# A long DFT in an fp32 kernel: the second transform of real and imaginary spectra as 64 x 64 products on quarters of TensorE, with mirrored sums in the outer steps

## Chip, cores, metric

One core of one Trainium2 chip. The metric is the device time of one execution in microseconds (us), the median of several executions. A "step" below is one block of 128 tokens of the main loop, which takes them in pairs; there are 196 steps, and I mark time by the start of each step's exponential on ScalarE.

## The reference

```python
X = np.fft.rfft(x, axis=1)                    # x: 8 x 3136 x 256, fp32
Y = X * (filt_r + 1j * filt_i)[None]
y = np.fft.irfft(Y, n=3136, axis=1)           # then 25088 tokens of 256
h = y @ w_in                                  # 256 -> 1024
sm = exp(h - max(h)) / (sum + 1e-9)
solu = h * sm
ln = (solu - mean) / sqrt(var + 1e-6) * g_ln
out = ln @ w_out                              # 1024 -> 256
```

The kernel does the length 3136 transform as 49 x 64: a first step over 49 rows (product `pa`), a second over 64 columns (`pb`), a product with the filter, and the way back (`pc`, then `py`). Entries 0 and 1 are transformed before the main loop. The other six are transformed in its gaps, in groups, while the loop does the two dense layers (`m` and `o`).

## The kernel before

Cuts are marked.

```python
# first step, entries 0 and 1: 16 tiles of x, 98 rows of 4 KB each, as 96 + 2 rows
def by_16(dmas, out, in_):
    n = out.shape[0] // 16 * 16
    dmas[0](out=out[:n], in_=in_[:n]);  dmas[1](out=out[n:], in_=in_[n:])
split((nc.sync.dma_start, nc.sync.dma_start), self.xs[i][0:NR],
      x[...].rearrange("(r n) c -> r n c", n=NH)[:, NCH * ch:NCH * ch + NCH, :])
# ...
def forward(self, i, ps):      # one residue s: 128 x 128 product, real and imaginary rows together
    nc.tensor.matmul(out=ps[:, ...], lhsT=self.des[i][:, j, 0, :], rhs=t2[...], start=True, stop=True)
def turn(self, i):             # ScalarE: swap the halves for the complex product
    nc.scalar.mul(turned[0:NQ], ps[NQ:P], -1.0);  nc.scalar.copy(out=turned[NQ:P], in_=ps[0:NQ])
def multiply(self, i, parts):  # VectorE: p = pb*f0 ; i = i*f1 ; p = p + i
# ... inverse: one 128 x 128 product into ps_t, one eviction by ScalarE
# after entries 0 and 1: ten products that nothing reads, so that TensorE's clock stays up
for j in range(10):
    nc.tensor.matmul(out=idle[:, 0, :], lhsT=tables[NS // NG - 1][:, 0, 0, :], rhs=last...)
# main loop: a unit of group n at step t
early[t]: forward, turn        products[0][t+1], products[1][t+1]: multiply
late[t + 1]: inverse           stores[t + 2]: store
```

PSUM in the main loop: `ps_b` one bank for pb, `ps_t` two for pa, py and pc, `ps_m` three for m, `ps_o` two for o.

Of the kernel before, what the change touches and what calls it, by code (L numbers as in the profile page):

```python
# [1 line left out]

# [15 lines left out]
P = 128  # L18
# [3 lines left out]

N1, N2 = 49, 64
NH = N2 // 2
NS, NQ = (N1 + 1) // 2, 64
NR = 2 * N1
NK = 4 * NS
NG = 5
# [10 lines left out]
    ((2,), (0, 6), (9, 13)),  # L39
    ((3, 4), (6, 13), (22, 25)),  # L40
# [6 lines left out]
def dft_tables():  # L47





    n1, n2 = np.arange(N1), np.arange(N2)
    s, q = np.arange(NS), np.arange(NQ)
    ph = 2 * np.pi * (np.outer(n1, s) % N1) / N1
    w = np.stack([np.cos(ph), -np.sin(ph)], 1)
    v = np.stack([2 * np.cos(ph), -2 * np.sin(ph)], 0)
    v[0, :, 0], v[1, :, 0] = 1.0, 0.0
    wf = np.zeros((N1, 2, NS, 2, 2))
    wi = np.zeros((NS, 2, 2, N1, 2))  # L60
    for h in range(2):
        wf[:, h, :, :, h] = w.transpose(0, 2, 1)
        wi[:, :, h, :, h] = v.transpose(2, 0, 1) / S

    kap = np.where(q[:, None] < 32, s + N1 * q[:, None], s + N1 * (95 - q[:, None]))
    sg = np.where(q < 32, 1.0, -1.0)[:, None]
    th = 2 * np.pi * ((n2[:, None, None] * kap) % S) / S
    c, sn = np.cos(th), np.sin(th)
    d = np.zeros((2, N2, NS, 2, NQ))
    d[0, :, :, 0] = c.transpose(0, 2, 1)  # L70
    d[1, :, :, 0] = sn.transpose(0, 2, 1)
    d[0, :, :, 1] = (-sn * sg).transpose(0, 2, 1)
    d[1, :, :, 1] = (c * sg).transpose(0, 2, 1)
    d = d.reshape(2 * N2, NS, 2 * NQ)
    f32 = np.float32
    de = np.stack([d, d.transpose(2, 1, 0)], 2)
    return wf.reshape(NR, NK).astype(f32), wi.reshape(NK, NR).astype(f32), de.astype(f32)


@with_exitstack  # L80
def kernel(
# [27 lines left out]
    f_dram = dram.tile([NS, NQ, 2, C], FP32, name="f_dram")  # L109
# [27 lines left out]
    def filter_rows(filt, quarter, s0, n):  # L137

        off, step = (s0 * C, C) if quarter % 2 == 0 else ((N1 - s0) * C, -C)
        return bass.AP(tensor=filt.tensor, offset=filt.offset + off,  # L140
                       ap=[[N1 * C, 32], [step, n], [1, C]])

# [3 lines left out]
    def by_16(dmas, out, in_):  # L146

        n = out.shape[0] // 16 * 16
        dmas[0](out=out[:n], in_=in_[:n])
        dmas[1](out=out[n:], in_=in_[n:])  # L150

    class Spectrum:



        def __init__(self, n, pools, load, load_de):
            self.n, self.entries, self.pools = n, GROUPS[n][0], pools
            self.load, self.load_de = load, load_de
            self.units = ([(s, 1) for s in range(NS)] if len(self.entries) == 2 else
                          [(s, min(2, NS - s)) for s in range(0, NS, 2)])  # L160
            self.xs, self.t1s, self.t2s, self.fs, self.prods, self.gs, self.des, self.turned = (
                {} for _ in range(8))

        def columns(self, ap, s, count):

            if len(self.entries) == 2:
                return ap[:, s, :, :].rearrange("b p c -> p b c")
            return ap[0, s:s + count, :, :].rearrange("s p c -> p s c")

        def fetch_x(self, i, split=by_16):  # L170
            b, ch = divmod(i, NH // NCH)
            self.xs[i] = self.pools["r"].tile([P, NCH, C], FP32, name=f"x_{self.n}_{i}", tag="r")
            split((nc.sync.dma_start, nc.sync.dma_start), self.xs[i][0:NR],
                  x[self.entries[b]].rearrange("(r n) c -> r n c", n=NH)[
                      :, NCH * ch:NCH * ch + NCH, :])
# [17 lines left out]
        def fetch(self, i, dma):  # L193
            s, count = self.units[i]
            cols = len(self.entries) * count
            self.t2s[i] = self.pools["t2"].tile([P, 2, C], FP32, name=f"t2_{self.n}_{i}", tag="t2")
            dma(out=self.t2s[i][:, 0:cols, :],
                in_=self.columns(d1[self.n], s, count))
# [7 lines left out]
        def forward(self, i, ps):  # L206
            s, count = self.units[i]
            t2, w = self.t2s.pop(i), len(self.entries)
            for j in range(count):
                nc.tensor.matmul(out=ps[:, w * j:w * j + w, :], lhsT=self.des[i][:, j, 0, :],  # L210
                                 rhs=t2[:, w * j:w * j + w, :], start=True, stop=True)
            self.prods[i] = ps

        def turn(self, i, **bufs):

            s, count = self.units[i]
            cols = len(self.entries) * count
            ps = self.prods[i][:, 0:cols, :]
            turned = self.pools["p"].tile([P, 2, C], FP32, name=f"i_{self.n}_{i}", tag="i",
                                          **bufs)[:, 0:cols, :]  # L220
            nc.scalar.mul(turned[0:NQ], ps[NQ:P], -1.0)
            nc.scalar.copy(out=turned[NQ:P], in_=ps[0:NQ])
            self.turned[i] = turned

        def multiply(self, i, parts):


            s, count = self.units[i]
            cols = len(self.entries) * count
            f = self.fs[i]  # L230

            def part(k):
                fk = f[:, 0:count, k, :]
                return fk.broadcast_to([P, cols, C]) if cols > count else fk

            if 0 in parts:
                pt = self.pools["p"].tile([P, 2, C], FP32, name=f"p_{self.n}_{i}", tag="p")[:, 0:cols, :]
                nc.vector.tensor_tensor(out=pt, in0=self.prods[i][:, 0:cols, :], in1=part(0), op=ALU.mult)
                self.prods[i] = pt
            if 1 in parts:  # L240
                turned, pt = self.turned.pop(i), self.prods[i]
                nc.vector.tensor_tensor(out=turned, in0=turned, in1=part(1), op=ALU.mult)  # L242
                nc.vector.tensor_tensor(out=pt, in0=pt, in1=turned, op=ALU.add)
                del self.fs[i]

        def inverse(self, i, evac):
            s, count = self.units[i]
            w = len(self.entries)
            pt, de = self.prods.pop(i), self.des.pop(i)
            ps = ps_t.tile([P, 2, C], FP32, name=f"pc_{self.n}_{i}", tag="t")  # L250
            for j in range(count):
                nc.tensor.matmul(out=ps[:, w * j:w * j + w, :], lhsT=de[:, j, 1, :],  # L252
                                 rhs=pt[:, w * j:w * j + w, :], start=True, stop=True)
            self.gs[i] = gt = self.pools["g"].tile([P, 2, C], FP32, name=f"g_{self.n}_{i}", tag="g")
            evac(out=gt[:, 0:w * count, :], in_=ps[:, 0:w * count, :])

        def store(self, i, dma):
            s, count = self.units[i]
            gt, cols = self.gs.pop(i), len(self.entries) * count
            dma(out=self.columns(d2[self.n], s, count), in_=gt[:, 0:cols, :])  # L260
# [569 lines left out]
```

## Time and profile before

| | before |
|---|---|
| median | 1786.94 us (1781.92 to 1788.27) |
| span of the profiled run, mean granted clock | 1779.0 us, 0.979 |
| first pb / idle products / first exponential | 70.4 / 141.0 / 194.5 us |
| steps 0 to 20, 20 to 94, 94 to 140 | 208.6, 620.8, 361.8 us |
| moved by DMA | 314.57 MB |

Up to 70 us x comes in and the first step runs; from 70 to 141 us VectorE does the complex products of entries 0 and 1; after that the main loop fills TensorE more and more.

### The profile page before, as it was taken

The page shows a single profiled execution, that of the slowest core. Times are in us where ns is not written, and L with a number is a line of the kernel's source. Part 1 is how long each engine was busy: PE and PEld are TensorE (multiplying, and loading weights), DVE is VectorE, ACT ScalarE, POOL GpSimd, SP SyncE. Part 2 cuts the span into 40 slices and gives each one's busy share as a digit, 9 for nine tenths or more (in the row PEclk, how much of TensorE's full clock was granted, in tenths as well). Part 3 has the DMA queues.
Part 4 walks back from the last instruction along what each step waited for, and adds up shares of the span by engine and source line. Part 5 has one row for each costly group of instructions (what it writes and reads, how often), then busy time and mean ns, then how long its engine had stood idle before and what let it go on. Part 6 is the DMA issues. An engine that isn't in the chain of part 4 may idle for free.

```text
span 1779.0 us, 28627 instructions
## 1 busy us (share of the span) xinstructions
PE 1671.6 (94%) x8692; PEld 1141.3 (64%) x8692; DVE 1244.1 (70%) x2586; ACT 1068.4 (60%) x1917; POOL 1093.9 (61%) x1290
## 2 busy tenths in 40 slices
PE   6688887899999999999999999989999999999996
PEld 1225445676666666766667667767777777777776
DVE  0793654578877875678798766767767777777773
ACT  2365555566767666666667666656666566655551
POOL 3242354677767775667877656546666656676664
PEclk9789998999999999999999999999999999999999
DMA  9876687897788865566777665557776444444443
GB/s 279 259 253 184 207 216 197 245 247 211 201 240 231 223 173 158 135 188 188 195 188 200 156 153 157 139 141 186 192 188 158 113 116 114 120 106 107 104 114 94
DMA packets 358120, 314.57 MB, mean 177 GB/s; under 512 B 60833, under 2 KB 318882, under 8 KB 357968
## 3 DMA queue, kind: packets, MB, share of 16 engines
q1 hardware_dynamic: 295664, 187.23, 41.0%
q0 software_dynamic: 29152, 86.45, 16.3%
q10 hardware_dynamic: 33152, 39.07, 7.7%
q8 instruction: 71, 1.16, 0.3%
q14 instruction: 81, 0.66, 0.1%
HBM read 131.65 MB, written 81.50 MB: 120 GB/s over the span
## 4 chain that ended last, share of the span: by engine, by line
PE 74%; DMA 11%; DVE 6%; ACT 3%; issue 3%; SPq 1%; POOL 1%; ACTq 0%; POOLq 0%; DVEq 0%
PE o L612 28%; PE m L500 28%; PE py L277 6%; PE pa L183 4%; PE pb L210 4%; PE pc L252 3%; DMA t<-d 2%; DMA x<-in_x_dram 2%; DMA d<-t 2%; DVE h L548 1%; DMA solu_t<-turn 1%; DMA f<-f_dram 1%; DMA de<-de_tbl 1%; ACT e L532 1%; DVE i L242 1%
## 5 line engine op out<-in xcount | busy, mean ns | idle before, releaser
L550 ACT ACTIVATE e<-h,nmu 128x1024 f32<-128x1024 f32 x196 | 225.3, 1150 | 307.9 <-DVE h L548 305.7
L612 PE MATMUL o<-w_out_sb,solu_t 128*128 128x128 f32 x3136 | 401.9, 277 | 3.0 <-DVE ot L629 1.9
L612 PEld LDWEIGHTS o<-w_out_sb,solu_t 128*128 128x128 f32 x3136 | 382.1, 193 | 33.6 <-issue 28.5
L500 PE MATMUL m<-w_in_sb,s 128*128 128x512 f32 x784 | 397.3, 598 | 6.3 <-ACT h L510 6.3
L612 PEld LDWEIGHTS o<-w_out_sb,u 128*128 128x128 f32 x2352 | 306.5, 192 | 148.7 <-issue 115.7
L612 PE MATMUL o<-w_out_sb,u 128*128 128x128 f32 x2352 | 312.7, 276 | 9.0 <-ACT ot L624 7.7
L479 POOL TENSOR_TENSOR u<-solu_t 128x512 f32<-128x512 f32 x98 | 153.9, 1571 | 265.8 <-DMA solu_t<-turn 152.3
L500 PE MATMUL m<-w_in_sb,y 128*128 128x512 f32 x588 | 304.5, 601 | 6.3 <-DVE h L521 3.5
L548 DVE SCALAR_TENSOR_TENSOR h<-e,rsum,h 128x1024 f32<-128x1024 f32 x196 | 291.8, 1489 | 7.1 <-DVE rsum L545 0.3
L631 DVE SCALAR_TENSOR_TENSOR ot<-o,rs_t,ot 128x128 f32<-128x128 f32 x294 | 102.5, 349 | 257.3 <-ACT ot L624 216.6
L479 POOL TENSOR_TENSOR u<-solu_t,u 128x512 f32<-128x512 f32 x98 | 144.7, 1477 | 173.1 <-PE o L612 171.6
L558 DVE STREAM_TRANSPOSE turn<-h 128x1024 f32<-128x1024 f32 x196 | 242.2, 1236 | 1.5
L524 DVE CUSTOM_DVE_ANT_0 h<-m,h 128x512 f32<-128x512 f32 x196 | 134.8, 688 | 138.3 <-ACT h L510 89.8
L510 ACT COPY h<-m 128x512 f32<-128x512 f32 x294 | 173.0, 589 | 91.3 <-PE m L500 77.9
L532 ACT ACTIVATE e<-h,nmax 128x1024 f32<-128x1024 f32 x196 | 224.5, 1146 | 0.0
L500 PEld LDWEIGHTS m<-w_in_sb,s 128*128 128x128 f32 x784 | 130.6, 192 | 79.2 <-issue 74.2
L277 PEld LDWEIGHTS py<-wi_t,t 100*128 100x128 f32 x1024 | 133.3, 195 | 62.9 <-issue 39.8
L183 PE MATMUL pa<-x,wf_t 98*100 98x512 f32 x256 | 141.7, 662 | 26.6 <-DMA x<-in_x_dram 20.7
L479 POOL TENSOR_TENSOR solu_t<-solu_t,solu_t 128x512 f32<-128x512 f32 x98 | 157.0, 1602 | 7.7
L277 PE MATMUL py<-wi_t,t 100*128 100x98 f32 x1024 | 134.9, 277 | 15.2 <-DMA t<-d 10.4
L500 PEld LDWEIGHTS m<-w_in_sb,y 128*128 128x128 f32 x588 | 99.3, 192 | 74.2 <-issue 50.8
L280 ACT COPY y<-py 128x392 f32<-128x392 f32 x128 | 108.2, 845 | 56.2 <-PE py L277 54.6
(72 smaller groups left out, 2049.1 us busy)
## 6 DMA issues: line engine op xcount, KB each, us to landing
solu_t<-turn SPq DMA_DIRECT2D x784, 128.0 KB
d<-g POOLq DMA_DIRECT2D x99, 256.0 KB, 5.5
out_dram<-ot SPq DMA_DIRECT2D x196, 128.0 KB
t<-d SPq DMA_DIRECT2D x56, 400.0 KB
d<-t POOLq DMA_DIRECT2D x96, 200.0 KB, 4.8
t<-d ACTq DMA_DIRECT2D x74, 256.0 KB
x<-in_x_dram SPq DMA_DIRECT2D x48, 392.0 KB
f<-f_dram POOLq DMA_DIRECT2D x104, 128.0 KB, 4.2
```

What stands on the lines that cost most here:

```text
L183: nc.tensor.matmul(out=ps[0:NK, j], lhsT=wf_t, rhs=self.xs[i][0:NR, 2 * u:2 * u + 2, :], start=True, stop=True)
L277: nc.tensor.matmul(out=psv[:, i, :], lhsT=t4s[e, ch][:, i, cb * P:cb * P + P], rhs=wi_t, start=True, stop=True)
L280: evac(out=y[:, cb, t0:t0 + S].rearrange("p (r n) -> p n r", n=NH)[:, n0:n0 + NCH, :], in_=psv)
L479: nc.gpsimd.tensor_tensor(out=out, in0=in0, in1=in1, op=op)
L500: nc.tensor.matmul(out=ms[j, bank], lhsT=lhsT, rhs=w_in_sb[:, w, :], start=m in (1, 2, 7), stop=True, skip_group_check=True)
L510: nc.scalar.copy(out=h_half(k, i), in_=ms[j, 0])
L524: nc.vector.tensor_tensor_reduce(out=h_half(k, i), in0=ms[j, bank], in1=h_half(*kept), scale=1.0, scalar=sofar, op0=ALU.add, op1=ALU.min, ...
L532: nc.scalar.activation(out=e, in_=hs[k], func=AFT.Exp, bias=nmaxs.pop(k)[:, 1:2], scale=-1.0, accum_out=esum)
L548: nc.vector.scalar_tensor_tensor(out=solu, in0=e, scalar=rsum, in1=solu, op0=ALU.mult, op1=ALU.mult, accum_out=nmu)
L550: nc.scalar.activation(out=e, in_=solu, func=AFT.Square, bias=nmu, scale=-float(DFF), accum_out=variances[g][:, i:i + 1])
L558: nc.vector.transpose(out=turns[g][:, :, i, :], in_=solus.pop(k).rearrange("p (f j) -> p f j", j=32))
L612: nc.tensor.matmul(out=pos[p, bank], lhsT=lhs[:, f, :], rhs=w[:, f, :], start=f == 0 and m in (1, 2, 7), stop=True, skip_group_check=True)
```

## The change

Intent: the second transform splits into real and imaginary inputs and outputs which only need 64 x 64 blocks when n2 is centred, so half of TensorE's work on it vanishes. Two residues are held as one unit, each of four quarters of the array does a 64 x 64 product at once, real and imaginary spectra go to two PSUM banks, and no turning on ScalarE is needed. To make n2 symmetric, the first step pairs column n with column 63 - n, so half of x is read mirrored.

Shortened; cuts are marked, and the last part names the calls without their arguments.

```diff
-                split((nc.sync, nc.sync), xs[0:NR], x....rearrange("(r n) c -> r n c")[:, 4ch:4ch+4])
+            for h, first, step in ((0, NCH * ch, C), (1, N2 - 1 - NCH * ch, -C)):
+                split(dmas, xt[N1 * h:N1 * h + N1],          # engines=15: 45 + 4 rows, twice
+                      bass.AP(..., offset=first * C, ap=[[N2 * C, N1], [step, NCH], [1, C]]))
...
+        def forward(self, i, pss):
+            for u in range(self.shape(i)[0]):        # residue: which half of the columns
+                for r in range(2):                   # real or imaginary: which half of the rows
+                    block = slice(NQ * r, NQ * r + NQ)
+                    self.product(i, pss[r][NQ * u:NQ * u + NQ], lambda v: de[block, v, 0, u, :],
+                                 t2[block, self.slots(u), :])
...
+            nc.vector.tensor_tensor(out=out, in0=re, in1=fk(part), op=ALU.mult)
+            nc.vector.tensor_tensor(out=term, in0=im, in1=fk(1 - part), op=ALU.mult)
+            add(out=out, in0=out, in1=term, op=(ALU.subtract, ALU.add)[part])
...  entries 0 and 1
+            sp.multiply(i, 0, nc.vector.tensor_tensor)
+            sp.multiply(i, 1, nc.gpsimd.tensor_tensor)
...
-            nc.tensor.matmul(out=idle[:, 0, :], lhsT=tables[NS // NG - 1][:, 0, 0, :],
+                             lhsT=tables[0][0:NQ, 0, 0]...,        # 64 rows
...  main loop: one pair of banks for pb and pc; m2 shares the banks of pa and py
+    ps_b = [pool(f"ps_b{u}", 1, PSUM) for u in range(2)]
...
+            early[t].append(forward into psum_pair("pb"))
+            late[t].append(multiply(i, 0, nc.vector.tensor_tensor))
+            products[t + 1].append(multiply(i, 1, nc.vector.tensor_tensor))
+            late[t + 1].append(inverse into psum_pair("pc"))
```

## The prediction

> **What bounds the kernel now.** I read the page first (busy shares), then the windows of 50 us, then the timeline of TensorE inside a full window, then the groups by form, and last the waits and the chain. The page, and two rows of its slices:
>
> ```profile
> PE 1671.6 (94%) x8692; PEld 1141.3 (64%) x8692; DVE 1244.1 (70%) x2586; ACT 1068.4 (60%) x1917; POOL 1093.9 (61%) x1290
> ...
> PE   6688887899999999999999999989999999999996
> ...
> DMA  9876687897788865566777665557776444444443
> ```
>
> TensorE (PE) is full from about the ninth slice (355 us) to the end, and not before, where the DMA engines are the fuller ones. The windows say it in numbers:
>
> ```profile
> 50.00:100.00 50.00, 35.27 (x62) 11.05 (x60) 44.59 (x82) 23.42 (x37) 15.78 (x24) 0.81 0.83 255
> ...
> 300.00:350.00 50.00, 45.28 (x216) 30.73 (x216) 29.73 (x56) 29.41 (x54) 29.80 (x40) 0.96 0.94 259
> ...
> 500.00:550.00 50.00, 50.00 (x255) 33.19 (x254) 37.73 (x77) 34.90 (x64) 36.39 (x45) 1.00 0.85 238
> ```
>
> The columns are PE, PEld, DVE, ACT, POOL, then clock, DMA share, GB/s. From 67 to 141 us (first and last pb and pc of entries 0 and 1) VectorE is the bound: 44.6 of 50 us. From 200 to 350 us transfers are. After 350 us PE is busy throughout. Busy time overlaps in pipelined matmuls, so I take costs from the starts in the timeline of PE:
>
> ```profile
> 461.28 1.02 PE L210 MATMUL pb<-t,de 128*128 128x512 f32 x2
> 462.14 1.95 PE L612 MATMUL o<-w_out_sb,solu_t 128*128 128x128 f32 x16
> 463.92 1.02 PE L500 MATMUL m<-w_in_sb,s 128*128 128x512 f32 x2
> 464.78 1.02 PE L500 MATMUL m<-w_in_sb,y 128*128 128x512 f32 x2
> 465.64 1.05 PE L612 MATMUL o<-w_out_sb,u 128*128 128x128 f32 x8
> 466.53 1.06 PE L612 MATMUL o<-w_out_sb,solu_t 128*128 128x128 f32 x8
> ```
>
> An fp32 product of 512 columns is two passes (x2), and the next starts 462.14-461.28 = 0.86 us later. A 128-column product is 0.89/4 = 0.22 us. A pair of steps needs 7 x 0.86 + 28 x 0.22 = 12.2 us, times 98 = 1200 us. In the window 500 to 550 all starts times these costs fill 97 to 98% of it. There, what PE saves or pays goes nearly one for one into the end time. The products under change, by form:
>
> ```profile
> L210 PE MATMUL pb<-t,de 128*128 128x512 f32 x150 | 82.2, 633 | 14.4 <-DMA t<-d 9.5 <-DVE p L238 4.7
> L252 PE MATMUL pc<-p,de 128*128 128x512 f32 x150 | 80.5, 620 | 10.8 <-DVE p L243 7.4 <-ACT g L255 3.5
> ...
> L210 PE MATMUL pb<-t,de 128*128 128x256 f32 x100 | 26.9, 391 | 9.8 <-issue 7.2 <-DMA de<-de_tbl 2.6
> L252 PE MATMUL pc<-p,de 128*128 128x256 f32 x100 | 25.9, 379 | 0.0
> ```
>
> So 75 products of 512 columns and 50 of 256, each way. 25 of the 75 belong to entries 0 and 1, before the main loop.
>
> **What the Trainium skill says.** (1) "TensorEngine Tiling (Array Packing)", Key Properties: tiles operate independently and can load weights and multiply in parallel, but a change of tiling mode drains TensorE. The kernel before uses only the full array (its forms show 98 to 128 rows), so its trace shows neither. (2) "TensorE: Matmul & The Clock Gate", Part 3: [...]tiles run together (4 x 4 tiles measured 10.6 times faster), but matmuls start strictly in program order. The trace agrees on order; that two passes of one fp32 product follow each other on the same weights' place at 0.43 us is what the trace adds, and no page says how a packed fp32 product behaves. (3) "PSUM — Partial Sum Buffer", on bank collisions: different row tiles must not write one bank at once. The change gives each row half its own bank, so it means them to overlap. (4) "DMA: Bandwidth & Descriptors", how many engines: a transfer uses a number of engines that divides its rows, so 49 rows would get 7, which is why the new x loads are cut 45 + 4 or go to the other queue. Of this the trace before shows only 96 + 2.
>
> **The change part by part.**
>
> *Products.* The flops of the second transform halve. In the main loop (entries 2 to 7): 50 x 0.86 + 50 x 0.43 = 64.5 us each way, 129 us both ways. (The 0.43 is an estimate, half of 0.86.) They become 2 x 13 + 2 x 7 = 40 units, 80 bursts both ways, so a burst replaces 129/80 = 1.61 us. A burst is four 64x64 products, two passes each. Columns stay, so a pass still takes 0.43 us. If all four quarters run together: 0.86 us. To that I add the entry and exit of the mode. An isolated product shows 1.02 us against 0.86 in a stream, so a drained pipe costs about 0.16 us, and a first weight load that nothing hides about 0.19 us at 128 columns, perhaps half for 64. Two changes: about 0.4 to 0.5 us (an estimate from those two). Burst 1.3 us, saving 0.3 x 80 = about 25 us.
>
> *Elementwise.* Before, per residue: two ACT halves (0.595 + 0.577) and three DVE ops (0.684 + 0.862 + 0.831 = 2.38 us). After, per two residues: four DVE products out of PSUM (4 x 0.684) and two sums (2 x 0.831) = 4.40 against 4.75 us, and no turning on ACT. In entries 0 and 1 one sum goes to GpSimd, so DVE has 13 x (2.74 + 0.83) = 46 us against 25 x 2.38 = 59 us. That stage lasts 74 us now, with DVE as its bound, so I expect 58 to 62 us: 14 us saved. Its transfers (6.5 MB in, 6.5 MB out at about 255 GB/s) need 51 us and allow it. In the main loop ACT and DVE are not the bound and the saving is worth little. The copies of the filter in the first stage (7.5 us of DVE and 43 us of its waiting for them) go too.
>
> *Transfers.* Filter and table are each read once for two residues: per group the table falls from 3.3 to 1.7 MB and the filter from 6.4 to 3.3 MB. The filter is also asked for a step earlier. The waits that this can take away:
>
> ```profile
> DVE p L238 <- DMA f<-f_dram: 25.8, 12, 7.7
> ```
>
> The chain has DMA f<-f_dram at 1% and de<-de_tbl at 1% of the span. Between 200 and 350 us transfers bind, and 5 MB fewer of 33 MB per 150 us are worth about 10 us. Against it, half of x now comes in rows of 1 KB instead of 4 KB, and 96 x loads are issued from GpSimd at some 0.57 to 0.75 us. It loses about 112 filter issues of 0.57 us (64 us), so its load is level. Net minus 10 us.
>
> *Buffers.* t2, p and g have one buffer each in the main loop, and m2 shares the two PSUM banks of pa and py. Units come every second step (6.1 us a step), so one buffer suffices if a transfer lands in some 8 us; m2 is freed within its step. I allow plus 5 us. The outer steps keep their shapes and cost the same.
>
> **Sum**, if quarters run together: -25 - 14 - 10 + 5 = -44 us, 1743 us.
>
> **The rivals.** (a) *Full overlap and cheap changes of mode*: a burst of 1.0 us saves 0.6 x 80 = 48 us, total about 1720 us. For it: the order of the products alternates row halves and the banks are split for it. (b) *Half overlap*: the second pass of a product waits for the first on its own quarter and holds up what is behind it on the same row half. Two row halves side by side then need three slots of 0.43 us = 1.29 plus 0.5 us of mode change = 1.8 us against 1.61, a loss of 15 us that the -19 of the rest about cancels: about 1783 us. For it: two passes per product, which the single-pass bf16 figures don't cover. (c) *Strict order over all quarters*: pass two of the first overlaps only pass one of the next, five slots = 2.15 us plus 0.5, and for units of single entries (four passes of 0.215 us on one quarter in a row) 2.8 plus 0.5. That is 52 x 1.04 + 28 x 1.7 = about 100 us lost, and nothing saved in the first stage: about 1870 us. For it: the rule of strict order. Against it: a change so carefully laid out for overlap would hardly have been kept. (d) *No overlap at all*: eight slots, 3.44 us, +180 us, 1950 us. (e) *The work is hidden anyway*: excluded for the main loop by a PE that is full after 350 us; true of some part of the first 350 us, where transfers bind.
>
> **Range and chances.** I give (a) and my sum together 0.5, (b) 0.33, (c) and (d) 0.17. Weighted towards the middle this gives 1750 us; 8 times in 10 between 1700 and 1830 us. Faster by 2% means below 1751 us: nearly all of the first case and a little of (b), 0.48. Within 2%: most of (b), the poorer end of my sum, 0.36. Slower: 0.16.
>
> **What will show it.** In the timeline of PE around a pb or pc burst: the time from its first start to the start of the next full-array product. 1.0 to 1.4 us supports the sum, about 1.8 (b), 2.6 or more (c). Starts of different quarters within a few ns of each other mean full overlap; starts 0.43 us apart mean strict order. The gap before the first full-array product after a burst measures the drain. The time from the first pb to the idle products should fall from 74 to about 60 us, DVE still its bound. The wait of DVE for f<-f_dram should be nearly gone, and megabytes moved should fall by about 20 (of 314.57). The span of a step after 1400 us (no spectra) must be unchanged, else the m2 bank is to blame. Wrong it would be made by a burst over 1.6 us; by waits of m for py's banks; or by GpSimd's queue delaying x loads and so pa.

## The result, and the profile after

The changed kernel took 1857.18 us (1849.66 to 1871.48, 4 runs), the kernel before 1787.61 us beside it: a ratio of 1.0402, 95% interval 1.0331 to 1.0473. A ratio is the mean time of one kernel's runs over that of the other's of the same rounds, so not quite the ratio of the medians. The predicted 1750 us and the range to 1830 us were both missed.

The page after, against the prediction's first fence: busy time, then three rows of the 40 slices.

```profile
PE 1676.2 (90%) x9192; PEld 1106.6 (60%) x9192; DVE 1229.4 (66%) x2583; ACT 948.0 (51%) x1715; POOL 1071.6 (58%) x1281
...
PE   4547978879999999999999999998999999999996
...
PEclk8677588889999999999999999999999999999999
DMA  8754457776668776556556565655656454444443
```

The same three windows (PE, PEld, DVE, ACT, POOL, then clock, DMA share, GB/s):

```profile
50.00:100.00 50.00, 24.80 (x34) 8.12 (x36) 33.52 (x67) 9.12 (x9) 10.73 (x17) 0.64 0.73 216
...
300.00:350.00 50.00, 38.14 (x183) 22.25 (x182) 20.53 (x42) 22.35 (x40) 33.05 (x43) 0.84 0.78 219
500.00:550.00 50.00, 47.24 (x267) 29.52 (x267) 40.20 (x82) 26.21 (x48) 31.27 (x38) 0.97 0.62 171
```

From 50 to 100 us DMA moves 216 GB/s instead of 255, and the clock is 0.64 instead of 0.81. In the window from 500 us TensorE was busy for 50.00 us before and is busy for 47.24 now: an engine that should have had spare time by doing less work has holes instead. The fifth slice of the clock (186 to 232 us) shows 0.5.

The groups of the quartered products, by form (busy and mean of one pass, then idle before them):

```profile
L244 PE MATMUL pb<-t,de 64*64 64x512 f32 x300 | 58.3, 659 | 10.2 <-DMA t<-d 9.5 <-ACT g L288 0.3 <-DMA de<-de_tbl 0.3
...
L244 PE MATMUL pc<-pi,de 64*64 64x512 f32 x150 | 46.4, 672 | 15.6 <-POOL pi L271 15.6
```

Busy time says little for four products that overlap; the timeline says what a burst costs. The kernel after, TensorE, start and duration:

```profile
510.60 0.65 PE L244 MATMUL pc<-pr,de 64*64 64x512 f32 x2
510.62 0.65 PE L244 MATMUL pc<-pi,de 64*64 64x512 f32 x2
511.08 0.59 PE L244 MATMUL pc<-pr,de 64*64 64x512 f32 x2
511.10 0.60 PE L244 MATMUL pc<-pi,de 64*64 64x512 f32 x2
511.62 1.13 PE L311 MATMUL py<-wi_t,t 100*128 100x98 f32 x8
```

All four first passes start within 20 ns, all four second passes 0.48 us later, and the next full-array product at 1.02 us. The m product before it held on for 0.95 us instead of 0.86 (the median burst of steps 20 to 94 takes 1.02 us too), so the burst costs 1.02 + 0.09 = 1.11 us where two full products cost 2 x 0.86 = 1.72. TensorE's part of the change works better than I predicted (1.3 us). The wait of VectorE for f<-f_dram is gone and 293.69 MB are moved, 20.9 fewer, both as predicted.

Here is where the 80.2 us between the two profiled spans come from; the last three columns are the runs c1, d3 and f1, explained below.

| stage, us | before | after | three edits | + two transfers | + evictions split |
|---|---|---|---|---|---|
| start to first pb | 70.4 | 99.2 | 100.1 | 93.2 | 90.5 |
| first pb to idle products | 70.6 | 75.4 | 59.5 | 53.6 | 54.1 |
| idle products to step 0 | 53.5 | 78.5 | 70.0 | 63.8 | 62.9 |
| steps 0 to 20 | 208.6 | 218.5 | 214.0 | 213.1 | 220.1 |
| steps 20 to 94 | 620.8 | 638.0 | 619.3 | 620.4 | 616.4 |
| steps 94 to 140 | 361.8 | 355.9 | 354.2 | 352.7 | 353.1 |
| step 140 to the end | 393.3 | 393.7 | 392.1 | 392.9 | 392.1 |
| span | 1779.0 | 1859.2 | 1809.2 | 1789.7 | 1789.2 |
| ratio of times | 1 | 1.0402 | 1.0152 | 1.0045 | 1.0022 |

Steps after 140 have no spectra and are unchanged, so m2's new banks are not to blame. 58.6 of the 80.2 us are lost before step 0, and 17.2 in steps 20 to 94, where TensorE has less to do. Each column is one trace. In six runs with the main loop of the changed kernel, steps 20 to 94 took 628.4 to 638.6 us, and in eight with the main loop of c1 619.3 to 627.5, so a few us in this row mean little.

### The profile page after: what moved, and what is told of

It is laid out like the page before. It is cut to its first block, busy times and chain, and to the rows that moved or that the text cites. A ratio compares the mean times of both kernels' runs of the same rounds, so it can differ in the third digit from the quotient of the medians.

```text
span 1859.2 us, 29143 instructions
## 1 busy us (share of the span) xinstructions
PE 1676.2 (90%) x9192; PEld 1106.6 (60%) x9192; DVE 1229.4 (66%) x2583; ACT 948.0 (51%) x1715; POOL 1071.6 (58%) x1281
## 2 busy tenths in 40 slices
DMA packets 356249, 293.69 MB, mean 158 GB/s; under 512 B 63105, under 2 KB 324290, under 8 KB 356096
## 4 chain that ended last, share of the span: by engine, by line
PE 62%; DVE 15%; DMA 11%; issue 4%; POOL 3%; ACT 3%; SPq 1%; ACTq 0%; DVEq 0%; POOLq 0%
PE o L653 25%; PE m L541 23%; PE py L311 6%; PE pa L219 4%; DMA solu_t<-turn 3%; DVE h L589 3%; DMA x<-in_x_dram 3%; DMA t<-d 2%; PE pc L244 2%; PE pb L244 2%; DVE turn L599 2%; DVE pr L271 1%; DVE pt L270 1%; DMA raw<-in_moe_w_out_dram 1%; DVE h L565 1%
## 5 line engine op out<-in xcount | busy, mean ns | idle before, releaser
L653 PE MATMUL o<-w_out_sb,solu_t 128*128 128x128 f32 x3136 | 406.9, 279 | 22.2 <-DVE ot L672 20.2
L541 PE MATMUL m<-w_in_sb,s 128*128 128x512 f32 x784 | 406.7, 612 | 3.9 <-ACT h L551 3.8
L653 PEld LDWEIGHTS o<-w_out_sb,u 128*128 128x128 f32 x2352 | 310.3, 193 | 147.7 <-issue 118.6
L519 POOL TENSOR_TENSOR u<-solu_t 128x512 f32<-128x512 f32 x98 | 149.8, 1528 | 282.2 <-DMA solu_t<-turn 176.2
L589 DVE SCALAR_TENSOR_TENSOR h<-e,rsum,h 128x1024 f32<-128x1024 f32 x196 | 283.5, 1446 | 7.4 <-DVE rsum L586 0.6
L219 PE MATMUL pa<-x,wf_t 98*100 98x512 f32 x256 | 150.1, 700 | 65.6 <-DMA x<-in_x_dram 54.1
L311 PEld LDWEIGHTS py<-wi_t,t 100*128 100x128 f32 x1024 | 142.4, 212 | 72.6 <-issue 51.5
L311 PE MATMUL py<-wi_t,t 100*128 100x98 f32 x1024 | 148.1, 297 | 18.0 <-DMA t<-d 15.1
L519 POOL TENSOR_TENSOR solu_t<-solu_t,solu_t 128x512 f32<-128x512 f32 x98 | 145.9, 1489 | 7.7
```

Source lines behind the costliest of these rows:

```text
L219: nc.tensor.matmul(out=ps[0:NK, j], lhsT=wf_t, rhs=self.xs[i][0:NR, 2 * u:2 * u + 2, :], start=True, stop=True)
L311: nc.tensor.matmul(out=psv[:, i:2 * NCH - i:2 * NCH - 1 - 2 * i, :], lhsT=t4s[e, ch][:, i, cb * P:cb * P + P], rhs=wi_t, start=True, stop= ...
L519: nc.gpsimd.tensor_tensor(out=out, in0=in0, in1=in1, op=op)
L541: nc.tensor.matmul(out=ms[j, bank], lhsT=lhsT, rhs=w_in_sb[:, w, :], start=m in (1, 2, 7), stop=True, skip_group_check=True)
L589: nc.vector.scalar_tensor_tensor(out=solu, in0=e, scalar=rsum, in1=solu, op0=ALU.mult, op1=ALU.mult, accum_out=nmu)
L653: nc.tensor.matmul(out=pos[p, bank], lhsT=lhs[:, f, :], rhs=w[:, f, :], start=f == 0 and m in (1, 2, 7), stop=True, skip_group_check=True)
```

## The experiments

My theory after the two traces: the products on quarters save what they should, and four losses of other engines and queues outweigh it: (1) x arrives later, (2) GpSimd's sum holds up the second transform of entries 0 and 1, (3) the clock falls to half after it, (4) VectorE's six operations of a unit in a row, three at the end of step t and three at the start of step t + 1, hold up the main loop. The general rival is that the losses have one cause, a mode of the array or a busier memory, so that mending one alone gives nothing.

### Four first looks at single causes

**a1_x_two_queues**: the mirrored half of x from ScalarE's queue.

```diff
-    sp.fetch_x(i, (nc.sync.dma_start, nc.sync.dma_start), partial(by_16, engines=15))
+    sp.fetch_x(i, ((nc.sync.dma_start,) * 2, (nc.scalar.dma_start,) * 2), ...)   # one pair for each half
```

> The changed kernel, with the mirrored half of each x tile of entries 0 and 1 issued from the ACT queue instead of SP. Four transfers per tile then no longer share one queue. Theory A (the head is late because each queue keeps only some eleven transfers in flight and a tile now takes four of them): the sixteenth first-step tile starts near 60 to 70 us instead of 88, the first pb near 75 to 82 us instead of 99, and the whole is some 15 to 25 us faster than the changed kernel (about 1835 us). Theory B (the head is late because the last 4 rows of each stored tile queue on GpSimd behind weight loads): nearly nothing changes, within 5 us.

Ratio 1.0438 (1.0384 to 1.0493), first pb at 97.0 us: no gain. It was a weak test: ScalarE asks for tile i only after it has evicted tile i - 1, because the load stands there in its program. The last run on the head mends this; what both share is said with the loads below.

**a2_store_act**: the four remaining rows of each store of the first step by ScalarE's queue instead of GpSimd's.

```diff
-    by_16((nc.scalar.dma_start, nc.gpsimd.dma_start), out, in_)
+    by_16((nc.scalar.dma_start, nc.scalar.dma_start), out, in_)
```

> The changed kernel, with the last 4 rows of each first-step store of entries 0 and 1 issued from the ACT queue like the other 96, not from GpSimd. Theory B: the first pb moves from 99 to 75 to 82 us and the whole gains 15 to 25 us. Theory A: the x tiles arrive as late as before; first pb stays above 92 us and the whole changes by less than 7 us.

1.0346 (1.0296 to 1.0395), first pb at 102.5 us. GpSimd's queue does not delay the head. The time is still some 10 us shorter, more than I expected: from first pb to the idle products this run took 66.7 us instead of 75.4, because 9.6 us in which VectorE unpacks the dense layers' weights there in the changed kernel lay before first pb in this run.

**a3_idle_full**: the ten idle products on 128 rows.

```diff
-            last = sp.prods[i][0]
+            if i == NP - 2:
+                last = sp.prods[i][0]
...
-    lhsT=tables[0][0:NQ, 0, 0]
+    lhsT=tables[0][:, 0, 0]
```

> The changed kernel, with its ten idle products run on 128 rows of the array again (operands of the last full unit) instead of 64. Theory C (idle products on half of the array do not bring the granted clock up, so they and the 128 products of the first back step run at half clock): idle products take 9 us instead of 14 to 16, the py products of entry 0 take 14 to 17 us instead of 27.5, the granted clock is 1.0 from there, and the whole gains 15 to 20 us. If the clock is low for another reason: the py products still take over 25 us and the gain is under 6 us.

1.0311 (1.0265 to 1.0356). The two windows are the ten idle products and the stretch after them (144 passes of py and eight of pa), first in the changed kernel, then in this run:

```profile
174.60:193.00 18.40, 17.82 (x23) 6.11 (x23) 0.00 (x0) 0.59 (x1) 3.21 (x4) 0.56 0.62 176
193.00:227.70 34.70, 34.70 (x154) 30.99 (x153) 0.00 (x0) 16.24 (x21) 6.85 (x13) 0.55 0.27 75
```

```profile
173.90:186.30 12.40, 12.27 (x22) 4.45 (x23) 0.00 (x0) 0.59 (x1) 3.25 (x4) 0.81 0.43 135
186.30:215.20 28.90, 27.34 (x152) 22.22 (x153) 0.00 (x0) 16.27 (x21) 6.76 (x13) 0.76 0.57 144
```

At a granted clock of 0.56 and 0.55 the same products take 18.4 and 34.7 us instead of 12.4 and 28.9. TensorE is busy all through both windows of the changed kernel and still isn't granted its clock: half clock runs from 176.6 to 224.4 us, the first 16.4 us of it during the idle products. With full rows it comes up within the idle products, at 178.5 us. It does not stay up, as I had expected: from 199.0 to 212.7 us it is at half again. So loss 3 is shown, and this edit mends part of it. It is no accident of one trace: in all seven runs with idle products on 64 rows and the sum on GpSimd they took 18.4 to 20.1 us.

**a4_part1_after_finish**: the second three VectorE operations of a unit not at the start of step t + 1 but at its early place, behind the operations that finish h and the outputs.

```diff
-    products[t + 1].append(lambda ...: sp.multiply(i, 1, nc.vector.tensor_tensor))
+    early[t + 1].append(lambda ...: sp.multiply(i, 1, nc.vector.tensor_tensor))
```

> The changed kernel, with the imaginary half of the filter product (three of a unit's six VectorE operations) moved from the start of a step to after that step's turn and finish. Theory D (six operations in a row, 4 us, delay the turn and the finish behind them, so the hidden products find their PSUM banks still full): PE's waits for nmax and for ot fall by more than half, and the whole gains 15 to 40 us, all of it between steps 10 and 140. If the loss comes from shared PSUM banks of m2 or from late x tiles: the waits stay and the gain is under 8 us.

1.0299 (1.0245 to 1.0353), steps 20 to 94 in 621.4 us instead of 638.0. That is below all six runs with the main loop as changed (628.4 to 638.6 us). Loss 4 is shown, and this is how it looks in the changed kernel: first VectorE, with the first of the six operations and what had to wait behind them, then TensorE at the same time.

```profile
894.89 0.68 DVE L269 TENSOR_TENSOR pr<-pb,f 128x512 f32<-128x512 f32 x1
...
898.74 1.24 DVE L599 STREAM_TRANSPOSE turn<-h 128x1024 f32<-128x1024 f32 x1
```

```profile
900.62 1.12 PE L541 MATMUL m<-w_in_sb,y 128*128 128x512 f32 x2 [1.68 <-DVE nmax L565]
```

Six operations hold VectorE from 894.89 to 898.74 us. Then come the transpose and the operation that empties the bank of m (nmax), and TensorE stands for 1.68 us. Over the window 465 to 1265 us the waits of TensorE in the changed kernel (us, times, longest) hold what the kernel before hardly had:

```profile
PE o L653 <- DVE ot L672: 14.4, 12, 3.4
PE m L541 <- DVE nmax L565: 11.2, 9, 2.0
```

The kernel before, over its window 395 to 1180 us, all that it has of these:

```profile
PE m L500 <- DVE h L521: 0.9, 2, 0.5
...
PE o L612 <- DVE ot L631: 0.2, 1, 0.2
```

To weigh this I took every TensorE start in steps 20 to 94 and summed the time to the next start. The products of the second transform hold 87.1 us before and 56.6 after: 30.5 saved. All others (o, m, py, pa) exceed their usual time (0.112 us a pass of o or py, 0.43 of m or pa) by 9.1 us before and by 56.1 after: 47.0 lost. 47.0 - 30.5 = 16.5, against 17.2 measured. With this edit the excess is 32.4 and the bursts hold 63.6: it takes away 23.7 us of waits and gives 7.0 back in the bursts.

### The next four

**b1_forward_late**: another way to spread VectorE's work, everything of a unit half a step later and two groups one step earlier.

```diff
-    early[t]: forward   late[t]: multiply 0    products[t+1]: multiply 1   late[t+1]: inverse
+    late[t]: forward    early[t+1]: multiply 0 late[t+1]: multiply 1       early[t+2]: inverse
```

> The changed kernel with the second transform of the main loop spaced out: forward products at the end of a step, the real filter half after the next step's finish, the imaginary half at that step's end, the inverse in the middle of the step after, a step's half between the eviction of pc and the next pb. Theory D (VectorE's six operations in a row) together with theory E (pb and pc share one pair of PSUM banks, so pb waits for ACT's eviction of pc, 36 us of PE waits in the run that only moved the imaginary half): PE's waits for nmax, for ot and for the eviction of pc all fall below 10 us each, steps 20 to 94 take about 31 us less than in the kernel before (52 bursts at 0.6 us), the whole is 25 to 45 us faster than the changed kernel. If the bursts do not really save 0.6 us each on the path: steps 20 to 94 take no less than the 621 us of the kernel before.

1.0464 (1.0433 to 1.0495). The waits only moved: m now waits for h, 36.4 us in the two rows of TensorE and its weight loads. So it isn't enough to cut the six in two. That they have to lie behind the finishing operations, as in a4, fits both runs, but this one moved the products and the inverse too.

**b3_x_natural**, wrong result: for entries 0 and 1 x in the old order, 98 rows of 4 KB as 96 + 2.

```diff
+    split(dmas, xt[0:NR], xb.rearrange("(r n) c -> r n c", n=NH)[:, NCH * ch:NCH * ch + NCH, :])
```

> Wrong result on purpose: the changed kernel reads x of entries 0 and 1 in the old rows (98 rows of 4 KB, cut 96 + 2, two transfers per tile) instead of mirrored (49 + 49 rows, half of them in runs of 1 KB, each cut 45 + 4). Theory F (the new form of the x loads is what makes the head late: short runs, and an uneven share of the engines): first pb at 72 to 82 us instead of 99, the whole 15 to 25 us faster. If the head is late because filters, tables and the projection weights are all asked for before the second transform: first pb stays above 92 us.

First pb at 72.0 us instead of 99.2, ratio 1.0267 (1.0249 to 1.0284). The way in which x is loaded makes 27.2 of the 28.8 us of loss 1.

**b4_x_main_sp**: in the main loop x from SyncE's queue instead of GpSimd's.

```diff
-    sp.fetch_x(i, (nc.gpsimd.dma_start,), whole)
+    sp.fetch_x(i, (nc.sync.dma_start,) * 2, partial(by_16, engines=15))
```

> The changed kernel with the x loads of entries 2 to 7 issued from SP again (45 + 4 rows per half) instead of from GpSimd. Theory G (x waits behind GpSimd's own waits for solu_t and o): PE's waits of pa for x in the main loop fall from about 30 us to under 15, steps 0 to 20 take 208 instead of 218 us, the whole gains about 10 us. Rival (SP is the busier queue, with solu_t and the output): x comes no earlier and the whole is the same or slower.

1.0437 (1.0404 to 1.047): no gain in the whole. But the stages moved: from the idle products to step 0 it took 70.8 us instead of 78.5, and the wait of pa for x there (5.1 us in the changed kernel) was gone; steps 0 to 20 then took 232.3 us instead of 218.5, with pa waiting 15.8 us for x and py 18.4 for t. So x does come late around the start of the main loop, and whether GpSimd's queue, which I had named as a danger, is the reason stays open.

**b5_head_sum_dve**: the sum of the imaginary half of entries 0 and 1 on VectorE.

```diff
-    sp.multiply(i, 1, nc.gpsimd.tensor_tensor)
+    sp.multiply(i, 1, nc.vector.tensor_tensor)
```

> The changed kernel with the imaginary sum of entries 0 and 1 on VectorE instead of GpSimd. Theory H (the sum on GpSimd slows VectorE's own sum from 0.83 to 1.57 us and stands on the path pb, pc): a unit's period goes from 4.85 to about 4.4 us, the stage from 71 to about 64 us, the whole gains 5 to 8 us. Rival (GpSimd takes real work off the bound engine): period about 5.1 us or more, the whole 3 us slower.

1.0208 (1.0187 to 1.023), the largest gain of a single edit. First pb to idle products falls from 75.4 to 59.4 us: VectorE does more and the stage is shorter. The lines show why. In the changed kernel, VectorE, GpSimd, and TensorE's wait in this stage:

```profile
125.65 1.52 DVE L271 TENSOR_TENSOR pr<-pr,pt 128x512 f32<-128x512 f32 x1
```

```profile
125.34 1.27 POOL L271 TENSOR_TENSOR pi<-pi,pt 128x512 f32<-128x512 f32 x1
```

```profile
PEld pc L244 <- POOL pi L271: 27.5, 12, 2.5
```

and the same sum of VectorE in this run, with no sum on GpSimd beside it:

```profile
120.62 0.68 DVE L271 TENSOR_TENSOR pr<-pr,pt 128x512 f32<-128x512 f32 x1
```

VectorE's sum takes 1.52 us while GpSimd's runs, and 0.68 alone; the operations that read one operand from PSUM stay at 0.68 in both. It was 1.57 in seven of the thirteen units, and 0.68 to 0.72 in the three whose sum hardly met GpSimd's. The Trainium skill says it: "GPSIMD Engine Reference", Specifications, gives GpSimd's access to SBUF as shared with VectorE, with contention where a VectorE instruction has two SBUF inputs. This is that case, and the trace agrees. Moving 0.68 us of work off VectorE cost it 0.84 us, and pc then waited for GpSimd with the next pb behind it in TensorE's order. The denser stage also kept the clock up: the idle products, still on 64 rows, take 10.0 us at a clock of 1.00. So 64-row products can run at a full clock; in the changed kernel, where it fell 2 us after they began, they did not bring it back. Note what VectorE did in this stage: its products and sums with the filter kept it busy for 47.9 us before, 49.2 in the changed kernel and 47.0 here. The stage is shorter than the 70.6 us before because 10.3 us of unpacking of weights lie in it instead of 18.1, and no copies of the filter (3.0).

### Three edits together, and what is left

**c1_three**: a3, a4 and b5 together.

> The changed kernel with three earlier edits together: both sums of the first stage on VectorE, the idle products on 128 rows, and the imaginary half of a unit's products at the next step's early place instead of at its start. Theory (three separate losses: second transform of entries 0 and 1, clock after it, VectorE's six products in a row in the main loop): the first exponential near 222 us as in the first edit, steps 20 to 94 in 611 to 622 us instead of 638, whole 1798 to 1808 us, ratio to the kernel before 1.005 to 1.015. The edits of the sums and of the idle products heal partly the same loss of clock, so their gains (36 and 16 us) do not add. Rival (the losses are one and the same, the total of transfers or VectorE's load): no better than the sums alone, 1817 to 1822 us.

1810.49 us, 1.0152 (1.0118 to 1.0186). Near the expected range; the first exponential is later than I said (229.6 against 222 us), steps 20 to 94 are as I said. Here the clock stays up through the idle products but falls at 183.4 us, and the first 128 passes of py take 23.7 us, where they took 16.4 before. The three losses are distinct, so the general rival falls; the edits of the sum and of the clock overlap.

**c2_pc_own_banks**: c1, and pc takes its accumulators from the banks of pa, py and m2.

```diff
-    sp.inverse(i, psum_pair(f"pc_{sp.n}_{i}"))
+    sp.inverse(i, [psum(f"pc_{sp.n}_{i}_{u}") for u in range(2)])
```

> The run with three edits, and in the main loop the way back (pc) takes its two accumulators from the pair that pa, py and m2 share instead of from the pair of pb. Theory (with the imaginary half late, pb waits for ScalarE's eviction of the unit before, because pb and pc share two banks): the wait of pb for g falls from some 36 us (both rows of the waits, matmul and weight load) to under 10, the time from an m product's start to the following pb burst no longer has an excess of 11 us over steps 20 to 94, these steps take 10 to 18 us less than with three edits, whole some 1780 to 1795 us. Rival (the banks of pa, py and m2 are as busy): the wait only moves to m2, pa or py, and the whole is the same as with three edits or slower.

1837.14 us, 1.0304 (1.0258 to 1.0351): the rival holds. One line of TensorE's waits in c1 (steps 20 to 94), two in this run:

```profile
PEld pb L244 <- ACT g L288: 25.2, 28, 2.2
```

```profile
PE py L311 <- ACT g L288: 17.9, 12, 2.4
PE pa L219 <- ACT g L288: 9.7, 5, 2.3
```

pb no longer waits for the eviction of the unit before, but py and pa do. A burst of four quarters fills two banks at once and holds them until ScalarE has emptied both; neither of the two places tried has that without a wait. The burst, 1.02 us, is no slower than the two evictions that empty it, 1.07 us.

**f1_evictions_split** (run last): c1 with d3's loads (below), and the second of a unit's two evictions on VectorE.

```diff
-    nc.scalar.copy(out=out[:, 0:w, :], in_=pss[u][:, 0:w, :])
+    (nc.vector.tensor_copy if u and self.n else nc.scalar.copy)(out=..., in_=...)
```

> The run with three edits and two transfers a tile, and in the main loop the second of a unit's two evictions (pc to g) on VectorE instead of ScalarE. Correct. In the run with two transfers the starts of m that stand before a pb burst are late by 12.2 us in all over steps 20 to 94, and the bursts hold 64.4 us instead of 57.2 at 1.1 us each. Theory (pb waits until ScalarE has emptied both banks of the pair): the 12.2 falls to 3 to 6 us, steps 20 to 94 take 612 to 617 us instead of 620, the whole 1780 to 1793 us, so the ratio to the kernel before 0.995 to 1.003. Rival (26 more evictions of some 0.65 us on VectorE bring its waits back: m for nmax, o for ot): steps 20 to 94 at 620 us or more, whole 1797 us or slower.

1792.01 us, 1.0022 (0.9997 to 1.0047), within my ranges, and steps 20 to 94 in 616.4 us. But not in the way I said: the bursts of pb hold 26.5 us instead of 32.6, since the second bank is free sooner (those of pc 33.6 instead of 31.8), while pb still starts 12.7 us late behind m in all, as the first bank still waits for ScalarE. Half of the theory is shown. The gain of 4 us over d3 is within what such traces differ by, and the two ratios are not told apart.

### What of the loads makes the head late

SyncE's issues of x at the start, before (L149 is the large part of a tile, L150 the rest) and after:

```profile
5.23 0.32 SPq L149 DMA_DIRECT2D x<-in_x_dram  x1
10.60 0.24 SPq L150 DMA_DIRECT2D x<-in_x_dram  x1
```

```profile
4.99 0.32 SPq L168 DMA_DIRECT2D x<-in_x_dram  x1
9.00 0.34 SPq L167 DMA_DIRECT2D x<-in_x_dram  x1
```

In both, SyncE first stops after nine or ten issues of x, long before the six tile buffers are full in the changed kernel, and each later wait is ended by the landing of an earlier transfer, of x or of a store:

```profile
SPq L168 <- DMA d<-t: 30.2, 11, 6.0
```

Before, nine transfers are four and a half tiles; after, with 45 + 4 + 45 + 4 rows, ten are two and a half. The trace says why it stops, which I overlooked. Each transfer names the semaphore that counts its landing. In the changed kernel the queues of SyncE and ScalarE share eight of them, and 47 of the 64 issues of x wait for the very semaphore that they name, so for the landing of the transfer that used it last, be it a load of x or a store of ScalarE's. Before it was 15 of 32. So the limit is eight transfers under way for two queues, and it lies in the program's semaphores; these runs show no limit of the issuer.

That is one theory (the number of transfers). Rivals: the runs of 1 KB, the cut into odd rows and its spread over DMA engines.

**c3_x_blocks**: c1, and the mirrored half in ascending blocks of 4 KB, put in order by two products with half their weights zero.

```diff
+    mirrored = (N2 - NCH - NCH * ch, C) if self.n == 0 else (N2 - 1 - NCH * ch, -C)
...
+    for h, n in ((0, 2 * u + v), (1, NCH - 1 - 2 * u - v)):
+        nc.tensor.matmul(out=ps[0:NK, j, C * v:C * v + C], lhsT=wf_half[h],
+                         rhs=self.xs[i][0:NR, n, :], start=h == 0, stop=h == 1)
```

> The run with three edits, and for entries 0 and 1 the mirrored half of x is read in ascending blocks of four columns (4 KB in a row, as the other half), the order being put right by making each product of the first step from two of 98 rows, of which each has half its weights zero. The result stays correct; TensorE does twice the work in the first 60 us. The cut of 45 and 4 rows stays. Theory (1 KB runs are what slows the head): the 16th tile of the first step starts at 62 to 75 us instead of 84 to 88, whole 10 to 25 us less than with three edits. Rival 1 (the cut into 49 rows, and so 45 and 4, is what slows it): no change at the 16th tile, 80 us or more. Rival 2 (TensorE becomes the bound with twice the products at a granted clock of 0.8): 16 tiles at 4 us or more each, no gain, TensorE busy over 90% from 10 to 80 us.

1832.81 us, 1.0255 (1.023 to 1.0281), 16th tile at 87.5 us. No gain, but some tiles follow each other at 3.5 us, which is TensorE's doubled work (16 passes of 0.22 us), so it doesn't settle the question.

**d2_x_blocks_wrong**, wrong result: the same loads with single products.

> Wrong result on purpose: the run with three edits, and the mirrored half of entries 0 and 1 is read in ascending blocks of 4 KB in the same four transfers a tile (45 + 4 rows twice), without putting the order right, so one product as in the changed kernel. Runs of 1 KB are gone, all else of the head is as in the changed kernel. If runs of 1 KB cost the time: 16th tile at 59 to 65 us. If the cut or the number of transfers does: 80 to 88 us. This takes TensorE's doubled products out of the result of the run with blocks.

16th tile at 78.4 us (one look, 1808.91 us).

**e1_x_cut_in_four**, wrong result: b3's rows of 4 KB, cut into 32, 32, 32 and 2.

```diff
+    for a in range(0, NR, 32):
+        dmas[0](out=out[a:min(a + 32, NR)], in_=in_[a:min(a + 32, NR)])
```

> Wrong result on purpose: the run with three edits, and x of entries 0 and 1 read as the kernel before reads it (98 rows of 4 KB), but cut into four transfers of 32, 32, 32 and 2 rows[...] instead of 96 and 2. The run that read the old rows as 96 and 2 had its 16th tile at 59.7 us, the run with 4 KB blocks in 45, 4, 45 and 4 at 78.4. If the number of transfers is the cause (SyncE has issued 8 to 10 when it first stops, whatever their size): 75 us or later. If it is the uneven spread[...], or the addresses: 58 to 64 us.

16th tile at 77.0 us, where the same rows as 96 + 2 had it at 59.7 (b3). This is the clean pair: same rows, same bytes, four transfers instead of two (e1 has c1's three edits besides, which all lie behind the head). From 10 to 50 us 6.6 packets of SyncE's queue were under way on average in b3 and 4.7 here. So about 17.3 of the 25.2 us to c1's 84.9 are the number of transfers, from one trace each. d2's 78.4 leaves 6.5 us for the runs of 1 KB, which is weakly shown: nine runs with the change's loads of the head untouched had the 16th tile anywhere from 79.9 to 92.3 us.

**d1_x_one_transfer** and **d4_x_one_wrong**: the two halves as one transfer a tile, with the doubled products (correct) and without (wrong).

```diff
+    bass.AP(..., ap=[[(N2 - NCH - 2 * NCH * ch) * C, 2], [N2 * C, N1], [1, NCH * C]])
```

> The run with three edits, and for entries 0 and 1 x comes in one transfer a tile (98 rows, mirrored half in ascending blocks of 4 KB, two products with half their weights zero put the order right, as in the run with blocks). The result stays correct. Theory A (the number of transfers: four a tile instead of two, with only so many under way at a time): the 16th tile of the first step starts at 62 to 72 us, where 3.4 us of TensorE a tile become the bound, the whole 1782 to 1795 us. Theory B (the cut into rows of 49, whatever the number of transfers, or TensorE's doubled products): 80 us or more, whole as the run with blocks, some 1810 to 1833 us.

> Wrong result on purpose: the run with three edits, and x of entries 0 and 1 in one transfer of 98 rows a tile in ascending blocks of 4 KB, without putting the order right, so one product a slice. It is the bound of what the loads can give: theory A: 16th tile at 57 to 63 us (the kernel before 59.0), first pb at 69 to 75 us, whole some 25 us below the run with three edits, 1780 to 1788 us, so equal to the kernel before within 0.5%. If one transfer on 14 engines of 16 is slower: up to 16/14 of that, 68 us.

1903.64 us (1.0632, 1.0572 to 1.0692), and 1886.1 us in one look. A miss: I had counted on 14 engines for 98 rows. d4's tiles come (164.0 - 18.0) / 15 = 9.7 us apart; 49 rows at the 0.16 us that a packet of this queue takes there are 8.0, and 1.7 of its packets were under way on average, so about two engines carried each transfer (an estimate from these numbers). The outermost dimension of the transfer is 2, not 98, and the page that I cited for 49 rows goes by this dimension. So the two runs test that page, not the number of transfers.

**d3_x_two_transfers**: c1, and each half in one transfer of 49 rows.

```diff
-    sp.fetch_x(i, (nc.sync.dma_start, nc.sync.dma_start), partial(by_16, engines=15))
+    sp.fetch_x(i, (nc.sync.dma_start, nc.sync.dma_start), whole)
```

> The run with three edits, and x of entries 0 and 1 comes in two transfers a tile of 49 rows each, not cut into 45 and 4; mirrored half in runs of 1 KB as in the change. Correct. If the number of transfers is the cause (A): 16th tile at 65 to 75 us, whole 10 to 20 us below the run with three edits. If rows of 49 spread over few DMA engines are worse (the reason I gave for the cut): 16th tile at 90 us or later, whole slower. If the runs of 1 KB are the cause: unchanged, 84 us.

1796.61 us, 1.0045 (0.9995 to 1.0095), the best result from one line. But the 16th tile is at 81.1 us, not at 65 to 75: fewer transfers, each of them longer. First pb comes 6.9 us earlier than in c1, and the second transform takes 5.9 us less, a gain at a place I did not expect. The trace explains it: of the unpacking of weights by VectorE, 10.3 us lie in that stage in c1 and 4.4 in d3, the rest before first pb.

**e3_x_two_queues_ahead**: c1, x on two queues as in a1, but asked for four tiles ahead.

> The run with three edits, and for entries 0 and 1 the unmirrored half of x goes by SyncE's queue, the mirrored half by ScalarE's, both asked for four tiles ahead. The first run with two queues let ScalarE ask for a tile only after it had evicted the one before, so it did not test a limit of one queue. Correct. If the limit is one queue's: 16th tile at 60 to 72 us, first pb at 75 to 85, whole 10 to 25 us below the run with three edits, 1785 to 1800 us. If it is shared by the queues (SyncE's waits name the stores of ScalarE's queue), or the loads wait for something else: 80 us or later, no gain.

1823.76 us, 1.0206 (1.015 to 1.0262). The 16th tile comes at 71.4 us, so two queues that ask early do bring x sooner, though they share the eight semaphores; what of it the queues do and what the asking ahead does is not told apart. First pb is at 98.1 all the same: ScalarE, which also evicts and stores, evicts the first tile at 20.2 us instead of 14.4. Loads gained, stores lost.

## Why the prediction was wrong

Point by point, by its own steps.

**Products: right in mechanism, too cautious in size.** All quarters run together; a burst costs 1.11 us, not 1.3. Steps 20 to 94 alone saved 30.5 us of TensorE. This was rival (a), and (b), (c) and (d) are refuted by the starts.

**Elementwise: wrong.** "That stage lasts 74 us now, with DVE as its bound, so I expect 58 to 62 us". It took 75.4 (and 70.6 before, counted from the first pb at 70.4 us, not at 67). The step that failed is "DVE has 13 x (2.74 + 0.83)": I took GpSimd's sum as free. It made VectorE's own sum 1.52 us instead of 0.68 and stood in pc's way. With the sum on VectorE the stage took 59.4 us, the number I had predicted, and that is luck. The 59 us of VectorE that I meant to cut, 25 x 2.38, came from means over the whole kernel; in this stage the same operations held it for 47.9 us, and six for each of 13 units hold it for 47.0. What fell was the unpacking of weights in the stage and the copies of the filter.

**Transfers: wrong sign.** "Net minus 10 us" counted bytes, and the bytes fell as counted. I named the runs of 1 KB as the cost and quoted the cut 45 + 4 as a remedy. The number of transfers was the larger cost, because they share eight semaphores: 17.3 us of the later 16th tile against 6.5 (weakly shown). First pb came 28.8 us later.

**Main loop elementwise: wrong.** "In the main loop ACT and DVE are not the bound and the saving is worth little." On average VectorE isn't (it was busy for 37.7 of 50 us before), but the order of its work decides when a bank of m or o comes free. The excess waits of steps 20 to 94, 47.0 us more than before, cost more than the 30.5 that the bursts saved. The six operations in one row are shown for 23.7 of them, by a4.

**Buffers: plus 5 us was the wrong place.** m2's banks and single buffers for t2, p and g did no harm that I can see. The pair of banks that pb and pc share did: c1's bursts hold 64.5 us instead of 56.6, and pb starts 12.0 us late behind m. It mostly shows when VectorE's waits are gone: in the changed kernel this was 3.3 us, before it 2.4.

**The clock: no step at all.** Idle products on 64 rows after a stage with holes left TensorE at half clock from 176.6 to 224.4 us. I had read the granted clock in the windows, and did not ask what the change does to it. With full rows these ten products took 12.4 us instead of 18.4.

My chances gave slower by 2% only to strict order of the quarters. No rival described a TensorE that saves its time and waits it away; the list of what would make it wrong named bursts over 1.6 us and m waiting for py's banks, which did not happen, and late x at pa, which did: pa waited 18.4 us for x from the idle products to step 20, against 3.9 before.

**Still open:** steps 0 to 20 stay 4.5 to 11.5 us longer than before in the repaired versions (c1, d3, f1), and the stretch from idle products to step 0 some 9 to 16 us longer. The traces say what TensorE waits for there. In d3 pa waits 8.8 us for x before step 0, where it had no such wait before, and 9.9 in steps 0 to 20 against 3.9; in f1 it is 8.2 and 10.9. In c1 7.3 us of the stretch are py at the fallen clock; in d3 and f1 the clock stayed up and py took 17.3 and 16.9 us. Why x comes late there no run isolates. The clock is also lower in steps 0 to 20 (0.90 in the changed kernel, 0.95 before), and of the excess waits that a4 leaves in steps 20 to 94 some are not traced. With four repairs, or five, the kernel equals the one before and does not beat it.

## What to carry to other kernels

When an engine that is full gets less to do, ask what frees the banks it writes, and in what order the other engines reach that work; their share of busy time does not tell. Work moved to an engine that seems to have time can slow the engine it is taken from, if both read the same memory. Count transfers as well as bytes: where a program shares a fixed number of semaphores among them, cutting each in two lowers the bytes that are under way.

## What the Trainium skill lacked or had wrong

- "TensorE: Matmul & The Clock Gate", Part 3, measures packing and states strict program order, but has nothing on packed fp32 products, which are two passes in these records: on four quarters all first passes start within 20 ns and all second passes 0.48 us later. In which order the program holds the passes is not in the trace, so this does not test the rule.
- "TensorEngine Tiling (Array Packing)", Key Properties, says a change of mode drains the array, without a size: here about 0.09 us into a burst and 0.16 us out (1.02 against 0.86 us).
- "TensorE: Matmul & The Clock Gate", Part 1, tells of activity that keeps the clock up, but not how the number of rows counts: ten idle products on 64 rows, TensorE being busy, took 18.4 us at a granted clock of 0.56, and on 128 rows 12.4 us at 0.81. It is not a matter of rows alone: after a denser stage the 64 rows ran at 1.00 in 10.0 us.
- Nothing is lacking in "DMA: Bandwidth & Descriptors", how many engines, for the miss with one transfer a tile: I had counted rows where the page goes by the outermost dimension, which was 2 (9.7 us a tile). That SyncE stops after some ten transfers is a matter of this program's eight semaphores and not of the chip.
